# Attention and MLP in one stream: the small tiles of slots 6 to 11 in one visit instead of two

## The chip, the core and the metric

The kernel runs on one core of a Trainium2 chip. The metric is the device time of one execution in microseconds. A core has five engines, each with a queue of its own that is worked off in order: TensorE (PE: matmuls and, as PEld, its weight loads), VectorE (DVE), ScalarE (ACT), GpSimd (POOL) and SyncE (SP), which here issues nearly all the DMAs. An instruction that waits holds up everything behind it on its engine.

## What is computed

Attention with normalised q and k (8 batches, 12 heads, 448 rows, 64 columns), and on its output, as 3584 rows of 768, an MLP:

```python
def rmsnorm(x, g):
    return x / np.sqrt(np.mean(x * x, axis=-1, keepdims=True) + 1e-06) * g
scores = scale * np.matmul(rmsnorm(q, g_q), rmsnorm(k, g_k).transpose(0, 1, 3, 2))
attn = np.exp(scores - max)            # max over the last axis
attn = attn / (sum + 1e-09)            # sum over the last axis
x = np.matmul(attn, v)                 # heads side by side: (3584, 768)
h = x @ w_in                           # (3584, 2048)
out = (h - np.tanh(h)) @ w_out         # (3584, 768)
```

The MLP's weights come as 64-bit floats and are rounded to 32 bits on the chip.

## The kernel before

**Slots.** A step is a pair of heads of one batch; there are 48, six for each batch. The kernel emits one slot for each step. Slots -3 to 5 (`first_slot`) are the first batch's attention alone. From slot 6 on, the attention of step s runs beside the MLP of the batch before: slots 6 to 11 (`early_slot`) beside the first batch's MLP, slots 12 to 47 (`slot`) beside the others'. The MLP is a Python generator, and `run(gap)` emits as many of its matmuls as fit into `gap`. A slot has four gaps: of 14 matmuls each (448 columns as two halves of 224, 7 products by Strassen's scheme in place of 8) in slots 6 to 8, and of 8 matmuls of 448 columns in slots 9 to 11. So the program order on each engine is written out by hand: what a slot emits between two `run` calls stands on every engine's queue between the MLP's instructions of those gaps.

**The attention of a step.** The 448 keys are three chunks of 128 and a last one of 64. `scores(s, c)` (L505) multiplies chunk c for two heads into two PSUM banks, and ScalarE takes the exponentials out of them (L510: tiles p for chunks 0 and 1, p_full for chunk 2, p_last for the last). `totals` (L578) multiplies the exponentials by ones for the sums, and VectorE takes the reciprocal (L583). Up to step 9 the sums are 16 matmuls over the chunks (32 records in the trace, two for each matmul); from step 10 on `add` and `add_last` (L527, L528, L535) first add the chunks up on VectorE, and 4 matmuls are left. `last_values` (L545) and `values` (L557) multiply by v into two banks, and `divide` (L619) scales them into xT on VectorE; for the last three steps of a batch GpSimd then makes the MLP's sums of blocks (L634 to L637). For the steps ahead, `turn` (L421, L425) transposes k and the scaled q on TensorE with two copies on ScalarE (L423, L429), `squares` (L123, L124) and `norm` (L133 to L135: two sums and two small steps on VectorE, two powers on GpSimd) make the root mean squares, and `norm_q` scales q's rows. `norm_q` is one VectorE instruction (L410), but for steps 9 to 14, which is in slots 6 to 11, it is eight small ScalarE instructions (L408).

**Banks.** Scores, sums, values and transposes of a slot share five PSUM banks ("sc") in strict rotation; the MLP has three ("mm"). Who takes a bank waits until the instruction that reads its old content is done.

**A visit** is the run of small tiles that TensorE works off between two stretches of MLP matmuls. An `early_slot` has two: totals(s) and the scores of chunks 0 and 1 of step s + 1 at its start; and after two gaps the scores of the last chunk, last_values(s), values(s), and the scores of chunk 2. The turn is a third, short one, after the first gap. Then add, add_last, norm and norm_q follow at 2.5, 3, 3.5 and 4 gaps. A `slot` has one visit at its start: the last chunk's scores, last_values(s), totals(s), values(s), and the scores of chunks 0, 1 and 2; the turn follows after one gap, and add, add_last, norm and norm_q after 0.5, 1.5, 2 and 3 gaps.

**The weights** are rounded while the first batch is under way, in 32 pieces, each with three steps: a on ScalarE (L71, L72), b on VectorE (L78, L79, L82) and c on GpSimd (L90). Three buffers hold the raw words; the DMA of piece n + 2 (L265, L269 from piece 16 on, 768 KB) is emitted with step a of piece n, and waits until step c of piece n - 1 has freed its buffer. Step b of a piece is emitted with step a of the next. When a piece is due is fixed by the MLP's position: the first layer has 28 products of six matmuls (0 to 27; seven for each of four sets), and `weight(due[...])` at a product's start emits what that list says (L643 to L645, L665). Pieces 16 to 23 come with products 18, 19, 21, 22, 23, 25, 26 and 27. Slot 8 begins two matmuls before the end of product 18, and slot 9 after product 27. In the second layer a piece comes with every sixth matmul (4.6 us). VectorE also makes Strassen's combinations of a set of pieces (L324), and a finished set is kept for the later batches by seven writes to DRAM (L332, 384 KB each), which stand in SP's queue between the loads; those of the last set stand behind the load of piece 21.

**The MLP's own instructions** on the other engines read the product's bank (`use`): copies on ScalarE (L729), sums on VectorE (L731, L733, L737, L738, L741, L745), the tanh on ScalarE (L711) and the subtraction on VectorE or GpSimd (L712). The second layer copies a bank on ScalarE (L846), transposes on VectorE (L770) and stores.

Of the kernel before, what the change touches and what calls it, by code (L numbers as in the profile page):

```python
# [20 lines left out]
NCH = 4  # L21
# [116 lines left out]
def bounded_path(tc, ctx, q, k, v, moe_w_in, moe_w_out, out, g_col, ident, ones, half_ones, neg_half, early):  # L138
# [17 lines left out]
    nc = tc.nc  # L156
# [3 lines left out]
    CP = S // NCH  # L160
    NP = H // 2
# [13 lines left out]
    KF, KR = S // P, S % P  # L175
# [32 lines left out]
    def load(s, names):  # L208
        b, hp = steps[s]
        for name in names:  # L210
            src = {"q": q, "k": k, "v": v}[name]
            if s == 0 and name != "v":
                t = early[name]
            else:
                shape = [CP, 2, NCH, D] if name == "q" else [P, NCH, 2, D] if name == "k" else [P, 2, NCH, D]
                t = nat.tile(shape, F32, name=f"{name}_nat", bufs=3 if name == "v" else 2)
                fetch(nc, name, t, src[b, 2 * hp : 2 * hp + 2], by_blocks(s))
            loaded[name, s] = t
# [174 lines left out]
    def squares(s):  # L393
        squares_of(nc, early["sq"], early["n"], loaded["q", s], loaded["k", s])
# [6 lines left out]
    def norm_q(s):  # L401
        rr, n = normed[s], early["n"]
        t = loaded.pop(("q", s))
        if NP + 3 <= s < 2 * NP + 3:
            for h in range(2):
                for c in range(NCH):
                    i = h * NCH + c
                    nc.scalar.mul(n[:, c, h], t[:, h, c], rr[:CP, 1, i : i + 1])  # L408
            return
        nc.vector.tensor_tensor(  # L410
            out=n.rearrange("p c h d -> p h c d"), in0=t,
            in1=rr[:CP, 1].rearrange("p (h c) -> p h c", h=2)[:, :, :, None].to_broadcast([CP, 2, NCH, D]),
            op=ALU.mult,
        )

    def turn(s, tk, tq):

        rr, n = normed.pop(s), early["n"]
        kn = loaded.pop(("k", s))
        for c in range(NCH):  # L420
            nc.tensor.transpose(tk[:, c * P : (c + 1) * P], kn[:, c].rearrange("p h d -> p (h d)"), ident)  # L421
        kT = qkp.tile([P, S], F32, name="kT")
        nc.scalar.mul(kT, tk[:, :S], g_col)  # L423
        for c in range(NCH):
            nc.tensor.transpose(  # L425
                tq[:, c * CP : (c + 1) * CP], n[:, c].rearrange("p h d -> p (h d)"), ident[:CP, :CP]
            )
        qT = qkp.tile([P, S], F32, name="qT")
        nc.scalar.copy(out=qT, in_=tq[:, :S])  # L429
        turned[s] = rr, kT, qT  # L430
# [5 lines left out]
    def by_blocks(s):  # L436
        return has(s) and steps[s][0] >= FIRST
# [51 lines left out]
    def sc_bank():  # L489
        return bank_of("sc")  # L490

    def scores(s, c):

        rr, kT, qT = turned[s]
        halves, keys, n = (1, P, S) if c < KF else (2, KR, HS)
        name, bufs = ("p", 2) if c < 2 else ("p_full", 1) if c < KF else ("p_last", 2)
        if c == 1:
            p = probs[s, 1] = probs[s, 0]
        else:
            p = probs[s, c] = pp.tile([P, 2, 2 if c < 2 else 1, n], F32, name=name, bufs=bufs)  # L500
        tiles = [sc_bank() for _ in range(2)]
        for i in range(halves):
            for h in range(2):
                r = slice(h * D, (h + 1) * D)
                nc.tensor.matmul(  # L505
                    tiles[h][i * keys : (i + 1) * keys, :n], lhsT=kT[r, c * P : c * P + keys],
                    rhs=qT[r, i * n : (i + 1) * n], start=True, stop=True,
                )
        for h in range(2):
            nc.scalar.activation(  # L510
                p[:, h, c if c < 2 else 0, :], tiles[h][:, :n], AF.Exp,
                scale=1.0 if rr is None else rr[:, 0, 2 * c + h : 2 * c + h + 1],
            )
# [23 lines left out]
    def last_values(s, av):  # L537

        v_nat, p = loaded["v", s], probs[s, KF]
        for n in range(2):  # L540
            keys = slice(n * KR, (n + 1) * KR)
            for m in range(2):
                for h in range(2):
                    r = (2 * m + h) * BL
                    nc.tensor.matmul(  # L545
                        av[n][r : r + BL, :HS], lhsT=v_nat[keys, h, KF, m * BL : (m + 1) * BL],
                        rhs=p[keys, h, 0], start=True, stop=False,
                    )
# [14 lines left out]
    def totals(s, dn):  # L563

        parts = [t[:, h, n * HS : (n + 1) * HS] for t in sums.get(s, ()) for n in range(2) for h in range(2)]
        parts = [(parts, [ones[:, :BL]] * 2)] if parts else []
        if not sums.pop(s):
            for p in full(s):
                parts.append(
                    ([p[:, h, n * HS : (n + 1) * HS] for n in range(2) for h in range(2)], [ones[:, :BL]] * 2)  # L570
                )
            last = probs[s, KF]
            parts.append(([last[:, h, 0] for _ in range(2) for h in range(2)], [half_ones[:, n] for n in range(2)]))
        for i, (moving, by) in enumerate(parts):
            for n in range(2):
                for h in range(2):
                    r = (2 * n + h) * BL
                    nc.tensor.matmul(  # L578
                        dn[r : r + BL, :HS], lhsT=by[n], rhs=moving[2 * n + h],
                        start=(i == 0), stop=(i == len(parts) - 1),  # L580
                    )
        rs = whole[s] = sp.tile([P, HS], F32, name="rs")
        nc.vector.reciprocal(rs, dn[:, :HS])  # L583
# [29 lines left out]
    def divide(s, av):  # L613
        b, hp = steps[s]
        rs = whole.pop(s)
        x = xT[b, hp] = xp.tile([P, S], F32, name="xT")
        for n in range(2):
            for m in range(2):
                nc.vector.tensor_tensor(  # L619
                    out=x[m * D : (m + 1) * D, n * HS : (n + 1) * HS],  # L620
                    in0=av[n][m * D : (m + 1) * D, :HS],
                    in1=rs[:, n * HS : (n + 1) * HS] if s >= FOLDED else rs[n * D : (n + 1) * D], op=ALU.mult,
                )
        for c in range(NCH):
            del probs[s, c]
        if hp < HC:
            return
        c = hp - HC
        if c == 0:
            tt[b] = tp.tile([P, 3, HC, HS], F32, name="tt", bufs=1)  # L630
        eng = nc.vector if b == 0 and c == HC - 1 else nc.gpsimd
        x11, x12, x21, x22 = (xT[b, r][:, n : n + HS] for r in (c, hp) for n in (0, HS))
        t1, t2, t4 = (tt[b][:, i, c] for i in range(3))
        eng.tensor_tensor(out=t1, in0=x12, in1=x11, op=ALU.subtract)  # L634
        eng.tensor_tensor(out=t2, in0=x22, in1=t1, op=ALU.subtract)  # L635
        eng.tensor_tensor(out=x12, in0=x22, in1=x12, op=ALU.subtract)
        eng.tensor_tensor(out=t4, in0=x21, in1=t2, op=ALU.subtract)  # L637
# [226 lines left out]
    def run(ns):  # L864

        spent[1] += ns
        while spent[0] + 1.0 < spent[1]:
            took = next(stream, None)
            if took is None:
                return  # L870
            spent[0] += took
# [4 lines left out]
    def gap_ns(s):  # L876

        if s < 2 * NP:
            return H_NS / 12 if s % NP < 3 else 4 * S / ENGINE_NS * CD * CF / 12
        return (H_NS + O_NS) / (4 * NP)  # L880

    def has(s):
        return 0 <= s < NS
# [32 lines left out]
        weight(EARLY * (s + 3) // (NP + 2))  # L916
        combine(2)

    def early_slot(s):
        gap = gap_ns(s)  # L920
        totals(s, sc_bank())
        if has(s + 1):
            scores(s + 1, 0)
            scores(s + 1, 1)
        if has(s + 2):
            load(s + 2, "v")
        run(gap)
        if has(s + 2):
            turn(s + 2, sc_bank(), sc_bank())
        if has(s + 3):  # L930
            squares(s + 3)
        if has(s + 4):
            load(s + 4, "qk")
        run(gap)
        if has(s + 1):
            scores(s + 1, KF)
        av = [sc_bank() for _ in range(2)]
        last_values(s, av)
        divide(s, values(s, av))
        if has(s + 1):  # L940
            scores(s + 1, 2)
        for work, n in ((add, 1), (add_last, 1), (norm, 3), (norm_q, 3)):
            run(gap / 2)
            if has(s + n):
                work(s + n)

    def slot(s):

        gap = gap_ns(s)
# [59 lines left out]
    for s in range(-3, NP):  # L1009
        first_slot(s)  # L1010
    for s in range(NP, NS):
        (early_slot if s < 2 * NP else slot)(s)
    run(1e9)


# [343 lines left out]
```

## Time and profile before

| what | value |
|---|---|
| median of 3 runs | 1420.25 us (1419.85 to 1420.42) |
| profiled execution | 1419.85 us; its span 1418.0 us |
| mean granted TensorE clock | 0.990 |
| slots 6 to 11 on TensorE, start of each | 86.80, 118.52, 148.73, 186.23, 220.40, 254.24 us |
| start of slot 12 | 286.19 us |
| VectorE busy from 103.3 to 133.5 us | 29.1 of 30.2 us |
| the chain that ended last | 87% TensorE, 5% VectorE, 3% DMA |

The profile gives busy times of each engine, groups of equal instructions with what they waited for, and a timeline. In a line of the timeline stand the start in us, the length, the engine, the source line, the operation, out<-in and how many records were merged; a bracket gives the idle time before the first of them and what ended it. A matmul of 32-bit floats is two records. From slot 13 on the kernel repeats about every 27.5 us with TensorE busy nearly without a break.

### The profile page before, as it was taken

How to read it: one execution, taken by the hardware profiler on the slowest of the kernel's cores; microseconds unless marked ns; L12 is line 12 of the kernel's file. 1: busy time of each engine (PE TensorE's matmuls, PEld its weight loads, DVE VectorE, ACT ScalarE, POOL GpSimd, SP SyncE). 2: the span in 40 equal slices, each digit the busy share in tenths (PEclk: the TensorE clock that was granted, in tenths of full speed). 3: DMA queues.
4: the chain of work that ended last, by engine and by line, in shares of the span. 5: the costliest groups of instructions: out<-in, count | busy, mean ns of one | idle time of the engine just before them, and what ended most of it. 6: DMA issues, size and time to landing. Idle time of an engine off the chain costs nothing.

```text
span 1418.0 us, 25611 instructions
## 1 busy us (share of the span) xinstructions
PE 1383.4 (98%) x9752; PEld 1163.8 (82%) x9752; DVE 919.3 (65%) x1565; ACT 478.8 (34%) x1118; POOL 523.2 (37%) x348
## 2 busy tenths in 40 slices
PE   6999899999999999999999999999999999999997
PEld 3568764478998898898889889988998988899997
DVE  3899788866655687567866668656875678633311
ACT  5765554234322333323332233223332233201100
POOL 4565565223521255214533236212452145401310
PEclk8999999999999999999999999999999999999999
DMA  8669788854566656665657666666566756365663
GB/s 183 156 193 238 244 259 224 236 182 133 173 168 158 171 166 163 173 184 156 176 152 195 157 157 178 178 155 165 163 172 171 178 159 186 113 187 170 191 191 94
DMA packets 355256, 249.73 MB, mean 176 GB/s; under 512 B 266484, under 2 KB 297396, under 8 KB 355124
## 3 DMA queue, kind: packets, MB, share of 16 engines
q1 hardware_dynamic: 355120, 248.00, 64.2%
q8 instruction: 79, 1.29, 0.4%
q14 instruction: 53, 0.43, 0.1%
q10 hardware_dynamic: 4, 0.00, 0.0%
HBM read 214.50 MB, written 33.42 MB: 175 GB/s over the span
## 4 chain that ended last, share of the span: by engine, by line
PE 87%; DVE 5%; DMA 3%; SPq 2%; ACT 2%; issue 1%; POOL 0%; ACTq 0%; DVEq 0%
PE mm L675 64%; PE sc L505 9%; PE sc L557 7%; PE mm L840 4%; PE sc L545 2%; DMA w_f<-w_in 1%; SPq L118 1%; DMA w_raw<-in_moe_w_out_dram 1%; DMA gT<-in_moe_w_in_dram 1%; DVE rs L583 1%; DVE w_out L82 1%; ACT sum_g L598 0%; SPq L265 0%; DMA k_nat<-in_k_dram 0%; POOL w_out L90 0%
## 5 line engine op out<-in xcount | busy, mean ns | idle before, releaser
L675 PE MATMUL mm<-xT,w_f 128*128 128x224 f32 x1392 | 275.6, 354 | 0.0
L675 PEld LDWEIGHTS mm<-xT,w_f 128*128 128x128 f32 x1392 | 262.1, 190 | 9.1 <-issue 7.2
L675 PE MATMUL mm<-gT,w_f 128*128 128x224 f32 x1344 | 263.0, 354 | 0.0
L675 PEld LDWEIGHTS mm<-gT,w_f 128*128 128x128 f32 x1344 | 252.8, 190 | 11.4 <-issue 6.5
L463 POOL TENSOR_TENSOR rr_mine<-rr_mine,neg_half 128x28 f32<-128x28 f32 x30 | 145.1, 4837 | 252.1 <-DVE rr_mine L462 252.1
L675 PE MATMUL mm<-tt,w_f 128*128 128x224 f32 x1044 | 209.4, 354 | 5.4 <-DVE gT L712 5.4
L675 PEld LDWEIGHTS mm<-tt,w_f 128*128 128x128 f32 x1044 | 196.5, 190 | 11.4 <-DVE gT L712 7.5
L675 PE MATMUL mm<-tg,w_f 128*128 128x224 f32 x1008 | 197.7, 352 | 0.0
L712 POOL TENSOR_TENSOR gT<-s,th 128x448 f32<-128x448 f32 x96 | 114.9, 1206 | 214.5 <-ACT th L711 213.6
L675 PEld LDWEIGHTS mm<-tg,w_f 128*128 128x128 f32 x1008 | 190.6, 190 | 0.0
L505 PE MATMUL sc<-qT,kT 64*128 64x448 f32 (+1 forms) x960 | 169.5, 501 | 10.1 <-ACT p_last L510 6.6
L505 PEld LDWEIGHTS sc<-qT,kT 64*128 64x128 f32 (+1 forms) x960 | 71.6, 168 | 82.3 <-issue 61.3
L598 ACT COPY sum_g<-sum 32x14 f32<-32x14 f32 x280 | 56.6, 202 | 224.7 <-DVE sum L594 219.0
L619 DVE TENSOR_TENSOR xT<-sc,rs_T 64x224 f32<-64x224 f32 x140 | 54.4, 389 | 68.6 <-PE sc L557 66.6
L635 POOL TENSOR_TENSOR tt<-xT,tt 128x224 f32<-128x224 f32 x23 | 17.1, 744 | 218.0 <-DVE xT L619 217.9
L510 ACT ACTIVATE p<-sc 128x448 f32<-128x448 f32 x120 | 55.5, 549 | 97.8 <-PE sc L505 97.8
L135 POOL TENSOR_TENSOR rr<-rr,neg_half 112x8 f32<-112x8 f32 (+1 forms) x36 | 59.8, 1682 | 65.2 <-DVE rr L134 65.0
L711 ACT ACTIVATE th<-s 128x448 f32<-128x448 f32 x96 | 55.0, 579 | 84.5 <-DVE s L737 36.1
L557 PE MATMUL sc<-p,v_nat 128*32 128x224 f32 x1344 | 79.9, 355 | 0.0
L840 PE MATMUL mm<-gT,w_out 128*128 128x448 f32 x192 | 74.6, 543 | 0.3 <-POOL w_out L90 0.3
L527 DVE TENSOR_TENSOR rows<-p 128x896 f32<-128x896 f32 x38 | 42.4, 1115 | 42.2 <-ACT p L510 42.2
L840 PEld LDWEIGHTS mm<-gT,w_out 128*128 128x128 f32 x192 | 35.7, 190 | 36.9 <-issue 34.9
(145 smaller groups left out, 1751.2 us busy)
## 6 DMA issues: line engine op xcount, KB each, us to landing
w_f<-w_in SPq DMA_DIRECT2D x196, 384.0 KB, 3.1
w_f<-w_out SPq DMA_DIRECT2D x147, 512.0 KB, 4.0
w_raw<-in_moe_w_out_dram SPq DMA_DIRECT2D x16, 768.0 KB, 5.1
out_dram<-th SPq DMA_DIRECT2D x192, 56.0 KB, 1.9
w_in<-w_out SPq DMA_DIRECT2D x21, 384.0 KB, 6.1
qk_nat<-in_q_dram SPq DMA_DIRECT2D x120, 56.0 KB, 2.4
qk_nat<-in_k_dram SPq DMA_DIRECT2D x120, 56.0 KB, 2.3
gT<-in_moe_w_in_dram SPq DMA_DIRECT2D x32, 192.0 KB, 4.4
```

The costliest lines, as they stand in the source:

```text
L135: nc.gpsimd.tensor_tensor(out=r, in0=r, in1=neg_half[:rows], op=ALU.pow)
L463: nc.gpsimd.tensor_tensor(out=mine, in0=mine, in1=neg_half[:, :1].to_broadcast([P, 2 * NJ]), op=ALU.pow)
L505: nc.tensor.matmul(tiles[h][i * keys : (i + 1) * keys, :n], lhsT=kT[r, c * P : c * P + keys], rhs=qT[r, i * n : (i + 1) * n], start=True, ...
L510: nc.scalar.activation(p[:, h, c if c < 2 else 0, :], tiles[h][:, :n], AF.Exp, scale=1.0 if rr is None else rr[:, 0, 2 * c + h : 2 * c + h ...
L527: nc.vector.tensor_tensor(out=t, in0=p[0], in1=p[1], op=ALU.add)
L557: nc.tensor.matmul(av[n][r : r + BL, :HS], lhsT=v_nat[:, h, c, m * BL : (m + 1) * BL], rhs=p[c][:, h, n * HS : (n + 1) * HS], start=False, ...
L598: nc.scalar.copy(out=acc[h * BL : (h + 1) * BL, g], in_=part[g * BL : (g + 1) * BL, h * NJ : (h + 1) * NJ])
L619: nc.vector.tensor_tensor(out=x[m * D : (m + 1) * D, n * HS : (n + 1) * HS], in0=av[n][m * D : (m + 1) * D, :HS], in1=rs[:, n * HS : (n + ...
L675: nc.tensor.matmul(bank[:, f * HS : (f + 1) * HS], lhsT=w[:, c * width + f, :], rhs=moving[p](c), start=(first and f == 0 and c == 0), sto ...
L711: nc.scalar.activation(th, h, AF.Tanh, bias=0.0, scale=1.0)
L712: eng.tensor_tensor(out=g[:, rows, cols], in0=h, in1=th, op=ALU.subtract)
L840: nc.tensor.matmul(bank[:, :S], lhsT=w_out_row(f, n // HC)[:, n % HC * P : (n % HC + 1) * P], rhs=g[:, f, :], start=(f == 0), stop=(f == C ...
```

## The change

In slots 6 to 11 `slot(s)` is called in place of `early_slot(s)`, which is gone. So the two visits of these slots become one at the slot's start, with totals between last_values and values, and add, add_last, norm and norm_q come earlier by 2, 1.5, 1.5 and 1 gaps; the loads of v, and turn, squares and the loads of q and k keep their places after no and after one gap. The MLP's stream, its due list and its gaps are as before. And norm_q's exception is gone: q's rows of steps 9 to 14, too, are scaled by the one VectorE instruction.

```diff
     def norm_q(s):
         rr, n = normed[s], early["n"]
         t = loaded.pop(("q", s))
-        if NP + 3 <= s < 2 * NP + 3:
-            for h in range(2):
-                for c in range(NCH):
-                    i = h * NCH + c
-                    nc.scalar.mul(n[:, c, h], t[:, h, c], rr[:CP, 1, i : i + 1])
-            return
         nc.vector.tensor_tensor(
...
-    def early_slot(s):
-        gap = gap_ns(s)
-        totals(s, sc_bank())
-        if has(s + 1):
-            scores(s + 1, 0)
-            scores(s + 1, 1)
-        if has(s + 2):
-            load(s + 2, "v")
-        run(gap)
-        if has(s + 2):
-            turn(s + 2, sc_bank(), sc_bank())
-        if has(s + 3):
-            squares(s + 3)
-        if has(s + 4):
-            load(s + 4, "qk")
-        run(gap)
-        if has(s + 1):
-            scores(s + 1, KF)
-        av = [sc_bank() for _ in range(2)]
-        last_values(s, av)
-        divide(s, values(s, av))
-        if has(s + 1):
-            scores(s + 1, 2)
-        for work, n in ((add, 1), (add_last, 1), (norm, 3), (norm_q, 3)):
-            run(gap / 2)
-            if has(s + n):
-                work(s + n)
...
     for s in range(NP, NS):
-        (early_slot if s < 2 * NP else slot)(s)
+        slot(s)
     run(1e9)
```

## The prediction

> **What bounds the kernel now.** I read four views in this order: the page's engine table, TensorE's timeline over slots 6 to 11, the waits there, and the timelines of the other engines around the largest wait.
>
> ```profile
> PE 1383.4 (98%) x9752; PEld 1163.8 (82%) x9752; DVE 919.3 (65%) x1565; ACT 478.8 (34%) x1118; POOL 523.2 (37%) x348
> ```
>
> TensorE is busy throughout, so only its own work and its waits can move the end. Its timeline (start, length, engine, line, operation; in brackets idle time and what ended it) has the largest wait of the six slots:
>
> ```profile
> 167.20 1.02 PE L505 MATMUL sc<-qT,kT 64*128 64x448 f32 x2
> 172.25 1.86 PE L505 MATMUL sc<-qT,kT 64*128 64x448 f32 x2 [4.03 <-ACT p_last L510]
> 174.03 3.19 PE L675 MATMUL mm<-tt,w_out 128*128 128x224 f32 x8
> ```
>
> Head 1's scores of chunk 2 stand 4 us: their bank still holds the last chunk's scores, which ScalarE has not read. Eight records that take 1.7 us elsewhere then take 3.2. Why ScalarE is late:
>
> ```profile
> 170.17 0.91 ACT L71 ACTIVATE w_out<-w_raw 128x768 f32<-128x768 f32 x1 [4.71 <-DMA w_raw<-in_moe_w_out_dram]
> 170.98 0.89 ACT L72 ACTIVATE w_raw<-w_raw 128x768 int32<-128x768 uint32 x1
> 171.77 0.77 ACT L510 ACTIVATE p_last<-sc,rr 128x224 f32<-128x224 f32 x2
> ...
> 185.63 0.93 ACT L71 ACTIVATE w_out<-w_raw 128x768 f32<-128x768 f32 x1 [3.87 <-DMA w_raw<-in_moe_w_out_dram]
> ...
> 190.21 0.94 ACT L71 ACTIVATE w_out<-w_raw 128x768 f32<-128x768 f32 x1 [2.34 <-DMA w_raw<-in_moe_w_out_dram]
> ```
>
> These are weight pieces 20, 22 and 23. The exponentials stand in ScalarE's queue behind a piece that has not landed. The SP queue says why pieces land late:
>
> ```profile
> 165.69 5.17 SPq L269 DMA_DIRECT2D w_raw<-in_moe_w_out_dram  x2
> 170.92 4.98 SPq L332 DMA_DIRECT2D w_in<-w_out  x7
> 176.17 9.14 SPq L269 DMA_DIRECT2D w_raw<-in_moe_w_out_dram  x2
> ```
>
> The load of piece 20 left when GpSimd had freed its buffer (step c of piece 17 ended at 165.67). Between the loads of 21 and 22 stand the seven 384 KB writes that keep a set, and they fill the engines (columns: us, busy times, then granted clock, DMA share, GB/s):
>
> ```profile
> 170.00:172.00 2.00, 0.00 (x0) 0.00 (x0) 1.93 (x3) 1.83 (x3) 0.47 (x1) 0.52 0.74 29
> ...
> 178.00:180.00 2.00, 2.00 (x12) 2.00 (x12) 0.00 (x0) 0.41 (x1) 0.00 (x0) 1.00 1.04 418
> ```
>
> So piece 22 was there only at 185.63, 15.1 us after the load of 21 was issued (170.5). VectorE is the third party: it is busy for 35.7 of the 36.5 us from 82 to 118.5, and reads the sums' bank late.
>
> ```profile
> 93.65 1.56 DVE L583 RECIPROCAL rs<-sc 128x224 f32<-128x224 f32 x1
> ```
>
> **TensorE's work, part by part** (start to start). Two visits cost 3.36 + 4.44 = 7.80 us in slot 7 (118.52 to 121.88, 133.50 to 137.94), 2.22 + 4.44 = 6.66 in slots 10 and 11, which have only eight sum records. Slot 12 already has the new order: one visit, 286.19 to 292.74 = 6.55 us. With slot 7's long product (1.65 in place of 0.40) that is 7.80. One visit saves 0.1 us in two slots, nothing in four. The MLP's 56 matmuls take 21.58, the last three slots' 32 take 24.46, a turn 0.82. Without a wait slots 6 to 8 would take 30.20 each, 9 would take 33.08, 10 and 11 31.83: together 187.3. They take 199.4 now. **12.1 us, nearly all of it waits,** are what can be won: 1.5 in slot 6, 7.3 in 8 (the wait and its slow records), 1.1 in 9, 2.0 in 10.
>
> **What moves on the other engines.** Eight L408 instructions a slot (1.93 to 2.03 us) leave ScalarE; one L410 comes to VectorE, 0.63 us alone and 1.06 on the mean. The four norm instructions on VectorE (1.7 us) with their two powers on GpSimd (3.2), the additions, the division and GpSimd's four L634-L637 (4 us) come earlier; the q, k and v loads keep their places among the matmuls, so SP's order hardly changes: the kept sets and the pieces are issued by the MLP's own order, which is not touched. I cost all of this at nothing by itself, since it runs beside the MLP's 22 to 25 us of matmuls in a slot; that cover is gone where VectorE has no idle time, which is slot 6 and the end of slot 8, and there the L410 costs up to its 1.06 and the norm up to 1.7, each once a slot. GpSimd's powers now come in the middle of the slot and can delay a step c behind them by 3.2; in slot 8 that is piece 20's, whose load then still leaves before piece 22 has landed. That is the added wait: in one visit the chunk 0 scores take the banks of the last chunk (need ScalarE's exponentials 3.9 to 5.1 us after the visit's start), chunk 1 takes the bank of the sums and the first values' (needs VectorE's reciprocal within 3.3 us), chunk 2 the second values'. Before, the sums' bank was due only at the turn, 6 us later, and a late ScalarE was covered by free banks.
>
> Slot 6: VectorE still divides slot 5 and rounds piece 6, so its reciprocal starts at 93.65 whatever TensorE does. TensorE would start 86.80, wait 0.7 for p_full (88.1), end values at 92.5 and chunk 0 at 93.4, wait for the reciprocal to 95.1 and for each division after it (0.8), and leave at 97.7: 10.9 in place of 7.8, **wait 3.1**.
>
> Slot 7: VectorE in order (L731, piece 11, one combination) starts its reciprocal at 123.8 and ends at 125.4; chunk 1 wants it at 126.2. No wait, 0.8 us to spare. Slot 8 likewise. Slot 8 starts at 86.8 + 33.3 + 30.2 = 150.3, and product 18 ends at 158.9; before it ended at 152.87, as half the small tiles came later.
>
> Slots 8 and 9: from the end of product 18 VectorE runs the same list as before (L741, piece 16, L737, L738, L745, piece 17), which began then without backlog. Shifted by 6.0, the load of piece 20 leaves at 171.7, that of 21 at 176.5, and after the seven writes piece 22 lands at 191.6. Then ScalarE has two halves of 22 (1.75), a tanh (0.55), 23 (1.75), a tanh: its exponentials of slot 9's last chunk start at 196.2 to 197, and slot 9's chunk 0 can start at 197.2. TensorE is at slot 9 at 180.5, at 185.6 if products 25 and 26 wait for VectorE's L731 and L733 (the norm now stands ahead of L733); its values end 5.2 later. So it waits 6 to 11 us, the two being the same lost time. The reciprocal, behind piece 22's rounding, ends near 198.2, the divisions at 199.8; the visit ends at 200.4. A wait of this length brought slow records before (1.3 + 1.5 us after 172.25); I take 1.4. MLP resumes as if at 201.8, slot 10 starts at 227.1, against 220.40 before. Slots 8 and 9 take 76.8 in place of 63.3: **wait 13.5**.
>
> Slots 10 and 11: pieces come 4.6 us apart and the visit stands 2.3 us behind one; slot 12's visit shows no wait. I take none (0 to 1.9).
>
> Sum: 187.3 + 3.1 + 13.5 = 203.9 against 199.4, +4.6 (unrounded). The profiled execution took 1419.85 (span 1418.0 and 1.85 around it), 0.4 below the median of the runs shown: **1424.4 us**. After slot 12 nothing differs but the start.
>
> **The clock.** After the 4.03 us wait the granted clock is 0.50, but it also is 0.50 from 34 to 40 us after an idle time of 1.70; after 0.89 (241 us) it stays 1.00. Slot 6's longest idle piece, 1.2 to 1.8, lies between: 0 to 2.8 us more; I take 0, the row nearest the lower end. The Trainium skill, "TensorE: Matmul & The Clock Gate", Part 1, has the clock halve after an idle window of about 3.4 us; by it slot 6 is free and the sum stays; by the 1.70 row it is up to 2.8 more. The trace speaks against the page here.
>
> **Bounds.** Lowest for slots 8 and 9: no contention with GpSimd, so step c of 17 ends 2.3 us sooner, 23 lands right behind 22, no slow records: 5.3 less, 1419.1. Highest: piece 23 keeps its old distance (196.2, exponentials at 198.5), slow records cost 2.8, slot 6 also 2.8, slot 10 keeps 1.9: 1432.
>
> **Rivals.**
> 1. The waits dissolve: piece 23 is through ScalarE before slot 9 wants chunk 0. Then only slot 6's wait remains: 1419.85 - 12.1 + 3.1 = 1410.9; without that too, 1407.8. For it: ScalarE loses 2 us of work a slot, and slot 8's bank wait goes for certain. Against: slot 9 wants chunk 0 at 185.7 (180.5 + 5.2), so piece 23, with 1.75 of its own, a tanh and an exponential behind it, must have landed by 183; it landed at 190.2 when its chain began 6 us sooner. This landing decides: each microsecond after 183 costs one.
> 2. The change does not do what it says: slot 8's 7.3 us reappear whole in slot 9 and nothing else: 1419.85 - 12.1 + 3.1 + 7.3 = 1418.2, no difference. For it: the same queue, the same cause. Against: the later chain.
> 3. VectorE becomes the bound of every visit. Its reciprocals started 4.6, 2.5, 1.0, 6.7, 3.7 and 2.8 us after the sums' product in slots 6 to 11; one visit allows 1.8. The excess in 7, 10 and 11 is 3.6: 1428.0, and over 1431 with a slow clock. Against: the norm no longer stands just ahead of it.
>
> **How the numbers follow.** Forecast 0.60 (own range 1419 to 1431, most above 1422.7), rival 1 0.18, rival 2 0.14, rival 3 0.08. The range 1411 to 1431 leaves out the waitless end and the slow-clock one. A measurement of this kernel tells 0.2% (2.8 us) from no change. Faster: rival 1 and a little of rival 2, 0.20. Same: most of rival 2 and the forecast's low end, 0.18. Slower: 0.62.
>
> **What would show it.** Right: slot 8 without a bank wait at chunk 2; a wait of 5 us or more at slot 9's chunk 0, ended by p_last behind L71 of piece 23, itself ended by a DMA; a clock of 0.50 after it; a wait of 1.5 to 2 at slot 6's chunk 1, ended by VectorE; slot 12 starting 3 to 7 us later. Wrong: slot 9's visit under 10 us, or piece 22 on ScalarE before 186; then rival 1 or 2. Waits ended by L583 or L619 in slots 7, 10 and 11 are rival 3.

## The result and the profile after

The changed kernel takes **1426.97 us** (median of 4 runs, 1425.68 to 1430.14); the kernel before, run beside it, 1420.34 (1419.85 to 1422.95). The ratio is 1.0046, 95% interval [1.0026, 1.0067]: slower by half a per cent, clear of the noise. The profiled execution is the longest of the four, 1430.14 with a span of 1428.3 us. The engine table of the page after:

```profile
PE 1388.2 (97%) x9752; PEld 1167.8 (82%) x9752; DVE 928.2 (65%) x1571; ACT 468.3 (33%) x1070; POOL 527.2 (37%) x348
```

TensorE has the same 9752 matmul records and 4.8 us more busy time: not more work, but records at half clock. Of the 9.8 us that the six slots below lose, 5.7 are idle time of TensorE (11.8 in place of 6.2) and 4.2 are longer records. ScalarE lost 48 instructions and VectorE won 6 (eight small scalings of q became one, six times).

The slots on TensorE (us; a slot starts with the first matmul of its visit):

| kernel | slot 6 starts | 6 | 7 | 8 | 9 | 10 | 11 | sum |
|---|---|---|---|---|---|---|---|---|
| before | 86.80 | 31.72 | 30.21 | 37.50 | 34.17 | 33.84 | 31.95 | 199.39 |
| after | 87.28 | 33.73 | 33.72 | 39.32 | 37.05 | 33.44 | 31.97 | 209.23 |
| e1_visit_only | 84.43 | 34.13 | 31.62 | 39.78 | 36.53 | 33.39 | 31.64 | 207.09 |
| e2_vector_q_only | 84.44 | 31.33 | 30.21 | 40.66 | 37.29 | 33.84 | 31.95 | 205.28 |
| e3_keep_late | 85.37 | 35.28 | 33.63 | 38.57 | 38.31 | 33.34 | 31.97 | 211.10 |
| e4_norm_late | 84.12 | 33.51 | 36.03 | 33.98 | 42.25 | 31.76 | 31.64 | 209.17 |
| e5_keep_and_norm | 87.06 | 33.44 | 36.09 | 33.97 | 39.60 | 31.64 | 31.63 | 206.37 |
| e6_ring_after | 85.19 | 34.06 | 35.31 | 39.72 | 34.04 | 33.36 | 31.96 | 208.45 |
| e7_ring_before | 85.40 | 31.62 | 30.21 | 34.54 | 34.28 | 34.40 | 31.94 | 196.99 |
| e8_one_visit_10_11 | 82.96 | 32.79 | 30.21 | 38.56 | 34.18 | 33.58 | 31.64 | 200.96 |
| e9_ring_norm | 84.33 | 33.57 | 35.98 | 34.01 | 41.20 | 31.65 | 31.64 | 208.05 |
| e10_ring_norm_sums | 84.01 | 34.84 | 36.96 | 34.72 | 40.08 | 31.77 | 31.78 | 210.15 |
| e11_sums_first | 87.83 | 35.24 | 33.55 | 38.59 | 38.79 | 33.37 | 31.98 | 211.52 |
| e12_ring_mixed | 87.09 | 31.76 | 30.22 | 36.21 | 34.28 | 33.60 | 31.64 | 197.71 |

What follows slot 12's start is the same in every one of these executions (span less start: 1131.5 to 1132.2 us), so the time is the start of slot 6 plus the six slots. The start moves between 82.96 and 87.83 though nothing before it differs: that is spread between executions, and it goes with the granted clock from 25 to 85 us (last section).

TensorE's timeline after, the groups that begin with a wait, and the records behind slot 7's:

```profile
95.35 2.79 PE L499 MATMUL sc<-qT,kT 64*128 64x448 f32 x8 [1.25 <-DVE rs L577]
...
128.18 3.16 PE L499 MATMUL sc<-qT,kT 64*128 64x448 f32 x8 [1.15 <-DVE rs L577]
131.27 3.02 PE L669 MATMUL mm<-tt,w_out 128*128 128x224 f32 x8
...
180.03 2.54 PE L669 MATMUL mm<-xT,w_out 128*128 128x224 f32 x12 [1.47 <-DVE s L725]
186.87 4.85 PE L669 MATMUL mm<-xT,w_out 128*128 128x224 f32 x12 [4.31 <-DVE s L727]
...
201.53 4.55 PE L499 MATMUL sc<-qT,kT 64*128 64x448 f32 x12 [2.41 <-ACT p_last L504]
...
236.74 2.78 PE L499 MATMUL sc<-qT,kT 64*128 64x448 f32 x8 [0.76 <-DVE rs L577]
```

Chunk 2's bank wait of 4.03 us in slot 8 is gone. In its place stand waits for the reciprocal in slots 6, 7 and 10, two waits of the MLP for VectorE at the end of slot 8 (L725 and L727 are the L731 and L733 of before), and slot 9's wait for p_last. A bracket isn't the whole price. Eight score records take 1.77 us undisturbed and 2.78 to 3.16 here, since they also follow VectorE's divisions one by one; and the twelve MLP records from 186.87 take 4.85 in place of 2.54, at half clock. The windows after show the latter for slots 7 and 8 (us, busy times of PE, PEld, DVE, ACT, POOL, granted clock, DMA share, GB/s):

```profile
128.00:130.00 2.00, 1.82 (x6) 0.67 (x6) 1.68 (x5) 0.86 (x2) 0.35 (x1) 1.00 0.50 123
130.00:132.00 2.00, 2.00 (x7) 0.91 (x7) 0.00 (x0) 1.26 (x3) 0.00 (x0) 0.60 1.01 227
132.00:134.00 2.00, 2.00 (x8) 1.82 (x7) 0.00 (x0) 0.53 (x2) 0.00 (x0) 0.55 1.03 214
...
188.00:190.00 2.00, 2.00 (x6) 1.80 (x6) 1.97 (x4) 0.81 (x2) 1.18 (x2) 0.50 1.03 416
```

ScalarE after, with pieces 20, 21, 22 and 23 and slot 9's exponentials:

```profile
181.10 0.94 ACT L71 ACTIVATE w_out<-w_raw 128x768 f32<-128x768 f32 x1 [4.62 <-DMA w_raw<-in_moe_w_out_dram]
...
187.09 0.92 ACT L71 ACTIVATE w_out<-w_raw 128x768 f32<-128x768 f32 x1 [3.81 <-DMA w_raw<-in_moe_w_out_dram]
...
196.51 0.94 ACT L71 ACTIVATE w_out<-w_raw 128x768 f32<-128x768 f32 x1 [7.70 <-DMA w_raw<-in_moe_w_out_dram]
...
198.92 0.96 ACT L71 ACTIVATE w_out<-w_raw 128x768 f32<-128x768 f32 x1 [0.16 <-DMA w_raw<-in_moe_w_out_dram]
...
200.99 0.83 ACT L504 ACTIVATE p_last<-sc,rr 128x224 f32<-128x224 f32 x2
```

The last chunk's exponentials stand behind piece 23, as foretold. VectorE after, ahead of slot 7's reciprocal and ahead of L727:

```profile
116.53 1.95 DVE L79 TENSOR_SCALAR w_f<-w_f 128x768 int32<-128x768 int32 x1
...
119.92 2.03 DVE L404 TENSOR_TENSOR n<-q_nat,rr 112x512 f32<-112x512 f32 x1
...
126.58 1.55 DVE L577 RECIPROCAL rs<-sc 128x224 f32<-128x224 f32 x1
...
184.05 1.45 DVE L134 TENSOR_SCALAR rr<-rr 112x8 f32<-112x8 f32 x1
...
186.20 0.62 DVE L727 TENSOR_TENSOR s<-mm,s 128x448 f32<-128x448 f32 x1
```

The new scaling of q takes 2.03 us, not 0.63, a rounding step (L79) 1.95 us where it takes 0.56 elsewhere, and the norm (183.33 to 186.29) stands just ahead of the sum that TensorE waits for.

### The profile page after: what moved, and what is told of

Read it like the earlier page. It is cut to its first block, busy times and chain, and to the rows that moved or that the text cites. A ratio compares the mean times of both kernels' runs of the same rounds, so it can differ in the third digit from the quotient of the medians.

```text
span 1428.3 us, 25550 instructions
## 1 busy us (share of the span) xinstructions
PE 1388.2 (97%) x9752; PEld 1167.8 (82%) x9752; DVE 928.2 (65%) x1571; ACT 468.3 (33%) x1070; POOL 527.2 (37%) x348
## 4 chain that ended last, share of the span: by engine, by line
PE 84%; DVE 7%; DMA 3%; SPq 2%; ACT 2%; issue 1%; POOL 0%; ACTq 0%; DVEq 0%; POOLq 0%
PE mm L669 61%; PE sc L499 9%; PE sc L551 6%; PE mm L834 4%; PE sc L539 1%; SPq L265 1%; DMA w_raw<-in_moe_w_out_dram 1%; DVE w_out L78 1%; ACT sum_g L592 1%; DVE rs L577 1%; DVE w_out L79 1%; SPq L118 1%; DMA gT<-in_moe_w_in_dram 0%; DMA w_raw<-in_moe_w_in_dram 0%; DVE w_out L82 0%
## 5 line engine op out<-in xcount | busy, mean ns | idle before, releaser
L706 POOL TENSOR_TENSOR gT<-s,th 128x448 f32<-128x448 f32 x96 | 117.3, 1230 | 215.6 <-ACT th L705 214.2
```

The source lines that it names most:

```text
L706: eng.tensor_tensor(out=g[:, rows, cols], in0=h, in1=th, op=ALU.subtract)
```

## The experiments

The theory was that one visit is late because it asks VectorE and ScalarE for their results sooner, while both follow the rounding of the weights. The rival was that the moved small work itself (the scaling on VectorE, the norm) is the cost. A third reading, which the runs then forced, is that VectorE's list is full, so that a wait that is taken away comes back elsewhere. "The changed kernel" and "the kernel before" say from which of the two an edit starts.

### The two halves of the change

**e1_visit_only**: the changed kernel with q's rows of steps 9 to 14 on ScalarE again.

```diff
         t = loaded.pop(("q", s))
+        if NP + 3 <= s < 2 * NP + 3:
+            for h in range(2):
+                for c in range(NCH):
+                    i = h * NCH + c
+                    nc.scalar.mul(n[:, c, h], t[:, h, c], rr[:CP, 1, i : i + 1])
+            return
```

> The one visit alone: the changed kernel, but q's rows of steps 9 to 14 are scaled by ScalarE again, as before the change. Theory V (VectorE, late with its rounding, holds the bank of the sums): the L404 scaling that stood 2.0 us in front of slot 7's reciprocal is gone, so the wait at slot 7's chunk 1 and its half clock go (3.5 us); slots 8 and 9 keep theirs: about 1423.5 us. Theory W (only the chain of weight pieces in slots 8 and 9 costs time, slot 7's wait is chance): as the changed kernel, 1427.

Measured: 1426.21 us (9 runs), ratio 1.0036 [1.0023, 1.005], nearer the second forecast than the first; the two intervals don't tell it from the changed kernel. In the trace slot 7's wait shrinks from 1.15 to 0.69 us, no slow records follow, and slot 7 is 2.1 us shorter. The waits of slots 8 and 9 stay. So the visits are most of the loss by themselves.

**e2_vector_q_only**: the kernel before with those same lines taken out, and the two visits kept.

> The scaling of q alone: the kernel before with its two visits, but q's rows on VectorE in all steps. Theories V and W both: nothing waits for VectorE's reciprocal for 6 us in this order, so within 1 us of the kernel before (1420 to 1421.5). Rival (moving 1 to 2 us a slot onto the busiest helper is what costs): 1424 to 1427.

Measured: 1425.53 us (11 runs), ratio 1.0029 [1.0019, 1.0039]. My expectation missed, and the number is the rival's: the scaling alone costs nearly as much as the visits alone, and the two together little more than either. TensorE's two large waits of this run, then the instruction that makes the second, then GpSimd beside it:

```profile
171.33 1.85 PE L499 MATMUL sc<-qT,kT 64*128 64x448 f32 x2 [5.86 <-ACT p_last L504]
...
198.57 0.66 PE L415 MATMUL sc<-ident,k_nat 128*128 128x128 f32 x4 [2.30 <-DVE rs L577]
```

```profile
195.03 2.02 DVE L404 TENSOR_TENSOR n<-q_nat,rr 112x512 f32<-112x512 f32 x1
196.97 1.54 DVE L577 RECIPROCAL rs<-sc 128x224 f32<-128x224 f32 x1
```

```profile
194.65 1.85 POOL L90 TENSOR_TENSOR w_out<-w_out,w_raw 128x768 int32<-128x768 int32 x1 [0.89 <-DVE w_out L82]
```

The scaling ends 0.55 us after GpSimd's step c (197.05 and 196.50). It does so ahead of slot 8's reciprocal in this kernel too (2.33 us, to 151.01; step c to 150.45) and ahead of slot 7's in the kernel after (2.03, to 121.95; step c to 121.40). Its own time alone is 0.63, so in all three it ran only once step c was through. In all three step c had started first. Where VectorE starts first, the scaling isn't held up. Both cases in the kernel after:

```profile
119.55 1.85 POOL L90 TENSOR_TENSOR w_f<-w_f,w_raw 128x768 int32<-128x768 int32 x1 [1.49 <-DVE w_f L82]
119.92 2.03 DVE L404 TENSOR_TENSOR n<-q_nat,rr 112x512 f32<-112x512 f32 x1
...
189.32 0.69 DVE L404 TENSOR_TENSOR n<-q_nat,rr 112x512 f32<-112x512 f32 x1
189.64 2.07 POOL L90 TENSOR_TENSOR w_out<-w_out,w_raw 128x768 int32<-128x768 int32 x1 [0.82 <-PE mm L669]
```

The Trainium skill, "SBUF — State Buffer", "SBUF: two separate sides", has a port pair that VectorE and GpSimd share as an exclusive lock, held for a whole instruction by the one that starts first, which an instruction of VectorE with two inputs in SBUF needs beside one of GpSimd that reads SBUF; these rows agree.

In slot 9 of e2 the 1.4 us too much go straight into the reciprocal that the turn's bank waits for (2.30 in place of 0.35). At slot 8's start the 1.7 us too much delay VectorE's list, and behind it piece 20: counted from slot 8's start ScalarE takes it at 23.3 us, before at 21.4, and the p_last wait grows from 4.03 to 5.86. After both, the windows at 172 to 178 and at 200 to 202 us have a clock of 0.50.

### One wait at a time

**e3_keep_late**: the changed kernel with the kept set's seven writes three pieces later in SP's queue.

```diff
-            if kept[1] < kept[0] and n >= 4 * kept[0] + 2:
+            if kept[1] < kept[0] and n >= (21 if kept[0] == SETS else 4 * kept[0] + 2):
```

> The changed kernel, but the seven writes that keep the last set stand behind the load of piece 23 in SP's queue, no longer between the loads of 21 and 22. Theory W: piece 22 reaches ScalarE at about 191 and not 196.5, piece 23 at about 197, the wait for p_last at slot 9 shrinks by 2 us or vanishes with its half clock: 1423.5 to 1425. Theory V (VectorE sets slots 8 and 9 too): unchanged, 1427.

Measured: 1427.87 us (11 runs), ratio 1.0044 [1.0029, 1.0059], no gain. Piece 22 does come sooner (ScalarE takes it at 189.71, not 196.51), but piece 23 then waits for its buffer until step c of piece 20 ends at 191.3, behind the norm's powers on GpSimd, and is there only at 196.90. Slot 9's wait goes from 2.41 to 1.60.

**e4_norm_late**: the changed kernel with norm half a gap later in slots 6 to 11.

```diff
-        if ahead:
+        if ahead and s >= 2 * NP:
             norm(s + 3)
         run(gap / 2)
         if blocks:
             turn_blocks(s + 2, 0)
+        if ahead and s < 2 * NP:
+            norm(s + 3)
```

> The changed kernel, but in slots 6 to 11 the norm (four VectorE instructions, two GpSimd powers) comes half a gap later, behind the next products' sums. Theory V: product 26 of slot 8 no longer waits 4.3 us for L727 behind the norm: about 3 us faster, 1424. Theory W: the wait goes over to slot 9's p_last, since piece 23 reaches ScalarE no sooner: 1426 to 1427.

Measured: 1428.70 us (6 runs), ratio 1.0053 [1.0038, 1.0067], above both forecasts. TensorE's timeline:

```profile
151.95 1.78 PE L669 MATMUL mm<-xT,w_f 128*128 128x224 f32 x8 [2.08 <-DVE s L725]
...
182.29 2.54 PE L669 MATMUL mm<-xT,w_out 128*128 128x224 f32 x12 [1.44 <-DVE s L727]
...
199.55 5.18 PE L499 MATMUL sc<-qT,kT 64*128 64x448 f32 x12 [6.84 <-ACT p_last L504]
```

L727 loses 2.9 us of its wait, slot 8 falls to 33.98 us, and slot 9's p_last wait rises from 2.41 to 6.84. Piece 23 decides when slot 9 can go on, wherever TensorE spends the time before. But the edit also has a price in slot 7, which takes 2.3 us more: there the later norm stands just ahead of L725 (148.50 to 151.37 on VectorE), and TensorE waits 2.08 us for it. The kernels e5, e9 and e10, which share this edit, have the same wait.

**e5_keep_and_norm**: both edits.

> The changed kernel with both: the kept set's writes behind the load of piece 23, and the norm half a gap later in slots 6 to 11. Each alone moved the wait and not the end. Theory W2 (the end of slot 9's visit is set by piece 23, whose load waits for two things in a row: step c of piece 20, behind the norm's powers on GpSimd, and the seven writes): together piece 23 reaches ScalarE 3 us sooner, 1423.5 to 1425. Rival (TensorE's time there is set by VectorE's own list): as each alone, 1427 to 1429.

Measured: 1427.09 us (5 runs), ratio 1.0044 [1.0027, 1.0062], the rival's number; slot 9 still waits 4.72 us for p_last.

### The transfers taken out of it

**e6_ring_after**: the changed kernel, with the raw words of pieces 20 to 23 landing in the buffers of the later batches' weight ring, which is idle until then, so that no load waits for step c.

```diff
+        elif 20 <= n < 24:
+            raw = ring[:, (n - 20) * 2 * DM : (n - 19) * 2 * DM].bitcast(I32)
...
-        return n - 3 < max(done[2], EARLY)
+        if 20 <= n < 24:
+            return done[1] >= 19
+        return n - (7 if 24 <= n < 27 else 3) < max(done[2], EARLY)
...
-            while done[0] < min(n + 4, PIECES) and place_free(done[0]):
+            while done[0] < min(n + (6 if n >= 18 else 4), PIECES) and place_free(done[0]):
```

> The changed kernel, but the raw words of pieces 20 to 23 land in the ring of the later batches' weights, which is idle then, and their loads leave in a row at product 21, waiting for no step c. Theory W2: ScalarE's waits for pieces in slot 8 (4.6, 3.8 and 7.7 us) shrink to 2 or less each and slot 9's wait for p_last goes: 1421 to 1424. Rival (VectorE's list sets these slots): 1426 to 1428.

Measured: 1427.20 us (11 runs), ratio 1.0047 [1.0032, 1.0061], the rival's number. TensorE and then ScalarE of this run:

```profile
179.85 2.54 PE L673 MATMUL mm<-xT,w_out 128*128 128x224 f32 x12 [1.48 <-DVE s L729]
186.72 4.85 PE L673 MATMUL mm<-xT,w_out 128*128 128x224 f32 x12 [4.34 <-DVE s L731]
...
200.53 2.77 PE L503 MATMUL sc<-qT,kT 64*128 64x448 f32 x8 [0.23 <-DVE rs L581]
```

```profile
190.97 0.89 ACT L71 ACTIVATE w_out<-w_f 128x768 f32<-128x768 f32 x1
...
194.96 0.79 ACT L508 ACTIVATE p_last<-sc,rr 128x224 f32<-128x224 f32 x2 [0.19 <-PE sc L503]
```

ScalarE now waits for TensorE and not the reverse, and slot 9 is 3 us shorter. Slot 8's two waits are unchanged to 0.03 us: they belong to VectorE alone, which has no idle time in this run from 163.95 to 201 us. The trace's six slots are only 0.8 us shorter, since after slot 7's wait for the reciprocal the half clock lasted 6.8 us (127.6 to 134.4) in place of 3.4, and the slot took 35.31.

**e7_ring_before**: the same edit in the kernel before.

> The kernel before, with the same ring buffers for pieces 20 to 23. Theory W2: the 4 us wait of slot 8 and its slow records (7.3 us) go, since piece 20 no longer comes late to ScalarE ahead of p_last: 1413 to 1415. Rival (TensorE was only as far ahead as VectorE's rounding allowed, and meets it again at the second layer's first rows or at slot 9's turn): 1417 to 1420.

Measured: 1418.68 us (11 runs), ratio 0.9979 [0.9965, 0.9993]. Slot 8's p_last wait falls from 4.03 to 1.68 us and the slot by 3 us; 0.6 come back in slot 10. The rival's number.

**e9_ring_norm**: the changed kernel with the ring landing and the late norm (the edits of e6 and e4).

> The changed kernel with both helps at once: the raw words of pieces 20 to 23 land in the idle ring (so that ScalarE's piece is never waited for) and the norm is issued half a gap later (so that it doesn't stand ahead of VectorE's rounding of piece 21's remainder). Theory that one visit is late in slots 8 and 9 through these two alone: slot 8 about 34 us instead of 39.3, slot 9 about 34 to 35 instead of 37.1, the six slots 201 to 203 us instead of 209.2, and the time 1420 to 1422. Rival, VectorE has no idle time from about 164 to 201 us, so that what slot 8 no longer waits comes back in slot 7 or at slot 9's visit: six slots 206 to 209, time 1425 to 1428. After the ring alone and the norm alone I hold the rival the likelier.

Measured: 1426.63 us (5 runs), ratio 1.0048 [1.0034, 1.0062], the rival's number. Slot 8 takes 34.01 as hoped, slot 9 takes 41.20. TensorE at slot 9's visit, then VectorE:

```profile
198.71 4.27 PE L503 MATMUL sc<-qT,kT 64*128 64x448 f32 x8 [4.01 <-DVE rs L581]
```

```profile
195.69 0.96 DVE L82 SCALAR_TENSOR_TENSOR w_out<-w_f,w_out 128x768 int32<-128x768 int32 x1
196.56 0.62 DVE L743 TENSOR_TENSOR s<-mm,s 128x448 f32<-128x448 f32 x1
197.10 1.55 DVE L581 RECIPROCAL rs<-sc 128x224 f32<-128x224 f32 x1
```

With transfers and norm out of the way VectorE runs without a pause from 162.62 us on and reaches slot 9's reciprocal at 197.10 (at 198.93 in e6), 6.4 us after the sums' product. Before, it came to it at 194.62, and TensorE had MLP products to do until the turn at 196.22 asked for that bank. This is what the two visits were good for.

### The order inside the visit

**e11_sums_first**: the changed kernel with the sums' product ahead of the last chunk's scores in slots 6 to 11.

```diff
-        if has(s + 1):
-            scores(s + 1, KF)
         dn = sc_bank() if s < FOLDED else None
+        first = s < 2 * NP
+        if first:
+            totals(s, dn)
+        if has(s + 1):
+            scores(s + 1, KF)
         av = [sc_bank() for _ in range(2)]
         last_values(s, av)
-        if s < FOLDED:
+        if s < FOLDED and not first:
             totals(s, dn)
```

> The changed kernel with the sums' product first in the visits of slots 6 to 11, nothing else. If the reciprocal's waits in slots 6 and 7 cost what they show: slot 6 shorter by about 1.2 us, slot 7 by 1.2 to 2.6, time 1423 to 1424.5. Rival, slots 8 and 9 hang on VectorE's list, which isn't shorter, so that TensorE arriving 2 to 4 us earlier waits 2 to 4 us longer at the rounded remainder: slots 6 and 7 shorter, slot 8 longer by the same, time 1426.5 to 1427.5.

Measured: 1431.46 us (5 runs), ratio 1.0075 [1.0061, 1.0089]: slower still, and neither theory's number. TensorE in slot 6, then VectorE:

```profile
95.91 4.29 PE L499 MATMUL sc<-qT,kT 64*128 64x448 f32 x12 [2.26 <-DVE rs L577]
```

```profile
94.29 1.56 DVE L577 RECIPROCAL rs<-sc 128x224 f32<-128x224 f32 x1
```

The reciprocal starts 6.46 us after the slot (94.29 - 87.83), as in the kernel after (93.74 - 87.28 = 6.46): VectorE's list sets it, not the product. But the sums now hold the first bank of the visit and no longer the third, so the rotation gives that bank to chunk 0's scores instead of chunk 1's: all twelve records wait (x12, after: x8), by 1.01 us longer (2.26 less 1.25).

**e10_ring_norm_sums**: the same in e9_ring_norm.

> The kernel with ring and late norm, and in slots 6 to 11 the sums' product goes first in the visit, ahead of the last scores, so that VectorE gets some 1.7 us more for the reciprocal before TensorE asks for its bank. Theory that the reciprocal comes too late by 0.7 to 1.3 us in slots 6, 7 and 10 and no more: no wait for the reciprocal there, 1 to 3 us less than the run without it (the waits of 1.25, 1.15 and 0.76 us, and a half clock after slot 7's). Rival, VectorE's lateness is only handed on to the next wait: no difference over 0.7 us between the two.

Measured: 1427.41 us (5 runs), ratio 1.0048 [1.0034, 1.0061], no gain. The waits for the reciprocal grow from 6.8 to 10.3 us in all, with all twelve records waiting as in e11.

### One visit where VectorE isn't late

**e8_one_visit_10_11**: the kernel before with one visit in slots 10 and 11 alone.

```diff
-        (early_slot if s < 2 * NP else slot)(s)
+        (early_slot if s < NP + 4 else slot)(s)
```

> The kernel before with one visit in slots 10 and 11 alone (two visits in 6 to 9, q's rows on ScalarE). Where no piece is late the one visit is worth 0.1 us a slot and takes slot 10's 1.9 us wait away, less a wait for the reciprocal of up to 1: both theories 1418.5 to 1420.5, no difference that can be told from the kernel before. Rival (one visit is dearer by itself): 1422 or more.

Measured: 1417.78 us (11 runs), ratio 0.9976 [0.9967, 0.9986], better than either forecast. In the trace slots 10 and 11 give only 0.26 and 0.31, and slots 6 and 8, which the edit doesn't touch, take 1.1 more each; what is gained lies before slot 6 (start 82.96), which it doesn't touch either.

**e12_ring_mixed**: the ring landing and that line.

> The kernel before with the ring landing and with one visit in slots 10 and 11 alone, q scaled on ScalarE throughout. If the two add: 0.2 to 0.6 us off the ring landing's 1418.7 by the two slots' own traces, 2.5 us off by the times of the run with one visit in slots 10 and 11: 1416 to 1418.5. If the ring already took the wait that one visit shortens: 1418.5 to 1420.

Measured: **1414.71 us** (7 runs, 1413.86 to 1418.76), ratio 0.9961 [0.9949, 0.9974]: the fastest version here, ahead of both kernels and below both forecasts. Its profiled execution is the longest of the seven, and its six slots take 1.7 us less than before's; the other 4 us of the median aren't in that trace. TensorE's two largest waits in it:

```profile
170.21 1.76 PE L509 MATMUL sc<-qT,kT 64*128 64x448 f32 x2 [1.66 <-ACT p_last L514]
...
224.34 3.79 PE L509 MATMUL sc<-qT,kT 64*128 64x448 f32 x12 [0.84 <-ACT p_last L514]
```

## Why the prediction was right, and where it was not

The forecast was 1424.4 and the median is 2.6 above it; the sign, the size and the main mechanism held. By its steps, from the profiled execution:

- **TensorE's work.** Right: 9752 records before and after, and where no wait stands the slot takes what was foretold (slot 11: 31.97, foretold 31.83).
- **Slot 6.** Right. The reciprocal starts at 93.74 (93.65), and the slot takes 33.73 (33.3).
- **Slot 7, "No wait, 0.8 us to spare".** This is the step that failed. The reciprocal starts at 126.58, not at 123.8, and the slot takes 33.72, 3.5 more. I had timed VectorE's list with the durations of before, where GpSimd stood elsewhere. The new scaling took 2.03, where I had 0.63 alone and at most 1.06, and an L79 at 116.53 took 1.95 (0.56 undisturbed), beside GpSimd's L706. That made a wait of 1.15 us; the divisions that the scores follow one by one and the half clock behind them cost the rest. e1 agrees as to the scaling: in its trace slot 7 is 2.1 us shorter.
- **The scaling of q "at nothing by itself".** Wrong, as e2 shows: alone it costs 0.29% [0.19, 0.39]. The upper bound of 1.06 us was a mean over all slots. Behind a step c that has started it takes 2.0 to 2.3, and in e2 it met one in two places where VectorE has no slack (151 and 197 us), in the kernel after in one (122 us).
- **Slots 8 and 9.** Right as a sum, 76.37 (76.8). Counted from slot 8's start, which came 4.4 us later than foretold, the chain held within 0.6 us: load of piece 20 at 176.65 (171.7), piece 22 on ScalarE at 196.51 (191.6), the exponentials at 200.99 (196.2 to 197). The loss stands at another place than the forecast put most of it: 5.8 us at products 25 and 26, 2.4 at slot 9. The text had named both as the same lost time, and e4 shows that a wait goes over from the one to the other: 2.9 less at L727, 4.4 more at p_last.
- **But what sets that loss is two chains, not one.** I held piece 23's landing for the cause. e6 removed it, and slot 8 stayed as it was; e9 removed the norm as well, and the wait went to the reciprocal. VectorE's list is a second bound of the same length.
- **Slot 10.** 1.6 us above the forecast, within its bound of 1.9: a wait of 0.76 for a reciprocal behind a transposition (L764), and slower scores behind it.
- **The clock.** Took 0 after slot 6's wait and 1.4 after slot 9's; it was 0 in slot 6 and came in slots 7, 8 and 9.
- **The signs.** Slot 8 has no bank wait at chunk 2, and the clock is 0.50 after slot 9's wait, as named. But that wait is 2.41 us and not 5 or more, slot 6's is 1.25 and not 1.5 to 2, slot 12 starts 10.3 us later and not 3 to 7, and the waits in slots 7 and 10 are those named for rival 3.

Rival 1 (waits dissolve) is refuted by e6 and e9: even with the pieces there, VectorE is not. Rival 2 put slot 8's 7.3 us whole into slot 9 and no more: slots 8 and 9 together lost 13.1, and it left out slot 7. Rival 3, VectorE late at every visit, had 0.08 and is nearer than I gave it: its waits came in slots 6, 7 and 10, and with the transfers helped also in 9, and its number, 1428.0, is nearer the median than mine.

The sum of terms misses by 5.3 us in the profiled execution (209.2 against 203.9), of which slot 7 is 3.5, slot 10 1.6 and slot 6 0.4. The median is nearer since that execution is 3.2 us above it, which is luck as far as anything here shows; whether the other three lacked slot 7's half clock no trace shows.

**Still open:** what sets the clock up to slot 6, and so how much of e8's gain belongs to its edit. The mean clock of e8's 11 runs is 0.9929, of the 27 runs beside it 0.9914; over 1418 us that is an estimated 2.1 us of its 2.9. For e12 the two are 0.9927 and 0.9925, so the clock doesn't account for its gain, though its one trace shows only 1.7 us of it in the slots.

## What to carry to other kernels

Joining two stretches of small matmuls saves TensorE next to nothing if the matmuls are the same, and it shortens the time the other engines have for their part; look up when each engine reaches the instruction that frees the bank, in its own queue, before moving the one who takes the bank. When a wait is removed and the time stays, count the idle time of the engine behind it: an engine without any will be waited for at the next place. Before work is moved to an engine, read its duration from rows where its neighbour is busy, not from its mean.

## What the runs showed of the hardware

- The scaling of q on VectorE, an elementwise product with two inputs in SBUF, takes 0.63 us alone. Where GpSimd's step c had started before it, it took 2.02 to 2.33 us and ended 0.55 us after step c; where it started before step c, it took 0.69 (after, 189.32 and 228.04). One scaling of e2 (119.90) started before step c but beside a power of the norm, which GpSimd was already at; it took 3.05 us and ended 0.55 us after step c.
- The granted clock fell to 0.50 for 3.4 us (130.4 to 133.8) after an idle time of 1.15 us (slot 7, after), but stayed at 1.00 after 1.25 us (slot 6, after). The length of the idle time alone doesn't decide it: at the same place, slot 6, it fell to 0.50 from 95.2 to 98.6 us in e3 after 1.17 us and stayed at 1.00 in e9 after 1.67. The stretches at half clock in the six slots of these traces last 3.4 us or a multiple of it (after: 3.4, 6.8 and 3.4). The Trainium skill, "TensorE: Matmul & The Clock Gate", Part 1, asks for a whole idle window of about 3.4 us; slot 7's row speaks against that, while its window running free of the work would fit such a scatter.
- The time up to slot 6 varied from 82.96 to 87.83 us with the same instructions, in step with the granted clock. From 25 to 85 us its mean was 1.00 in e8 (start 82.96), 0.97 in the seven executions that start at 84.01 to 85.37, 0.94 in e7 (85.40), and 0.91 in before, after, e5, e11 and e12 (86.80 to 87.83). What sets that clock the runs do not tell.
